# A routing gate moved off TensorE in an attention and two-layer mixture kernel, with a new order for the attention stage

## The chip, the cores and the metric

One core of one Trainium2 chip runs the whole program. The metric is the device time of one execution in microseconds (us). The engines are TensorE (PE, with its weight loads listed as PEld), VectorE (DVE), ScalarE (ACT), GpSimd (POOL) and the DMA queues that SyncE (SP), ScalarE and GpSimd fill.

## What is computed

```python
attn = softmax(rot(q) @ rot(k).T / 8) @ v          # 4 batches, 8 heads, 576 positions, 64 wide
x = attn, as 2304 tokens x 512
logits = x @ w_gate + modality_bias[modality_id]   # 8 experts
x = gate_w * (relu(x @ w1[e]) @ w2[e])             # e = argmax per token, hidden size 1024
do = x @ moe2_w_skip > 0
logits2 = x @ moe2_w_gate                          # 8 columns, with the skip column 9
out = x + do * gate_w2 * (relu(x @ w1b[e2]) @ w2b[e2])
```

Everything is float32. The first mixture (moe1) computes every token, the second (moe2) only those whose skip product is positive. Which tokens go to which expert is known only on the chip.

## The kernel before

**Attention.** Sixteen pairs of heads go through a software pipeline. Every step of it (loads, rotation, transposes, scores, exponentials, products) is a small function, and `attention` gives each a place from the table `POS` (lines 39 to 82): place = 10 x pair + offset. All steps are sorted by place and issued in that order, so the table sets the order in every engine's queue. GpSimd does the rotation (`rope`, L330 to L336), the residues of v (L347) and, every four pairs, the routing of one batch for moe1 (`route1` to `route4p`) and five indirect scatters into the list of moe1 (`scatter1`, L807). Constants are steps too: `constants1` loads the modality bias to one partition (`mbr`, L230) and `constants2` spreads it to 128 partitions with a GpSimd `partition_broadcast` (L240). `moe1_ahead1` to `moe1_ahead3` pick the expert with most tokens, load its first weights into `raw1` and gather the first tokens. Matrix products split each float32 operand into a rounded part and a residue: "hi" on ScalarE, "lo" on VectorE.

**moe1.** Blocks of 256 tokens, two by certain choice, then a list in DRAM order of experts; 9 blocks always run, the rest under nested run-time branches (`nest`, L1288). Here ten run. `body(i)` (L1212) does on TensorE: four groups of the first product (`mm1`, L1094, 24 matmuls each into one of two `psM` banks), the second product of half 0 (`mm2`, L1143, 24 matmuls into `psY`), the transposes of the next block's tokens (`xt`, L1073), the second product of half 1. Each group of `mm1` is followed by relu on ScalarE (L1102) and its residue on VectorE (L1107). Weights of a new expert are split by L982/L986 (first matrix) and L995/L998 (second) when the expert changes.

**The second gate** is `epi(i, t, stage)` for half t of block i. Stage 0 scales `psY` to `x2` on ScalarE (L1160) and takes index, validity and token number on GpSimd (L1161 to L1163). Stage 1 transposes `x2` in four TensorE transposes (L1168), copies them (L1170) and scatters `x2` to `out`. Stage 2 multiplies with the 9 gate columns in four float32 matmuls (L1176, eight PE instructions) and finds the expert on VectorE (L1178 to L1190). Stage 3 counts with two small matmuls (L1193, L1194). Stage 4 computes the slot (L1197 to L1205) and scatters token and weight into the list of moe2. Half 0 runs its stages within its own block, between the pieces of `mm2` of half 1. Half 1 runs them in the next block, one after each group of `mm1`; for the last block they run in the first block of moe2 (`last`).

**moe2** takes blocks of 128 tokens (L1367, L1407), ten here: four of one expert, then one per expert nearly. It has two slots of raw weights, `slots2 = [(raw1, raw2), (raw1b, raw2b)]`. The first expert's weights go to slot 1 on ScalarE's queue during block `sure - 2` of moe1 (`moe2_load`), the second expert's to slot 0 on SP's queue in the last block of moe1 (`moe2_second`, L1334).

Of the kernel before, what the change touches and what calls it, by code (L numbers as in the profile page):

```python
# [39 lines left out]
    load=-36.7017, rope0=-33.9451, rope1=-30.111, v_hi=-21.4821, v_lo=-18.1897,  # L40
    qk_tr0=(-30.6061, -30.6042, -30.5936, -30.1223), qk_tr1=(-28.4904, -28.4904, -28.4848, -28.4848),
    qk_tr2=(-29.2463, -29.2463), qk_hi0=-29.4052, qk_hi1=-27.2491, qk_hi2=-29.202, qk_lo0=-29.1934, qk_lo1=-26.9027,
    qk_lo2=-28.9941, stackq=-25.8754, stackk=-23.011, stack2=-22.5711,
    s_mm0a=(-22.0577, -22.0577, -22.0577, -22.0577), s_max0a=-21.4825, s_exp0a=-20.8972,
    s_mm1a=(-21.3076, -21.3076, -21.3076, -21.3076), s_max1a=-20.1346, s_exp1a=-19.5976,
    s_mm2a=(-22.2316, -22.2316, -22.2316, -22.2316), s_max2a=-21.7162, s_exp2a=-21.4126,
    s_mm3a=(-20.5225, -20.5225, -20.5225, -20.5225), s_max3a=-19.2489, s_exp3a=-17.295,
    s_mm0b=(-14.3536, -14.1043, -14.0042, -13.9921), s_max0b=-12.9587, s_exp0b=-12.9046,
    s_mm1b=(-13.0069, -12.9105, -12.9105, -12.9105), s_max1b=-12.8704, s_exp1b=-12.8563,
    s_mm2b=(-15.4526, -15.4526, -15.4386, -15.4386), s_max2b=-14.6158, s_exp2b=-14.0784,  # L50
    s_mm3b=(-16.5055, -16.5055, -16.5055, -16.5055), s_max3b=-15.336, s_exp3b=-15.2119,
# [12 lines left out]
    t_lo1b=-6.1978, pv1b=(-5.2632, -4.5696, -3.9061, -3.5847), t_mm2b=(-11.6405, -11.6405, -11.6405, -11.6405),
    t_hi2b=-11.3076, t_lo2b=-11.3076, pv2b=(-6.5077, -6.5077, -6.2903, -6.172),
    t_mm3b=(-10.8705, -10.8705, -10.8705, -10.8705), t_hi3b=-9.8594, t_lo3b=-9.5279,
    pv3b=(-5.2659, -5.2659, -5.2659, -5.2659), pv4b=(-3.1789, -3.0274), o_evb=-3.008,
    o_mmb=(-2.908, -2.9041, -2.9041, -2.8421, -2.8421), o_normb=-2.5794,
    t_mm4=(-12.3715, -12.3715, -12.3715, -12.3715), t_hi4=-11.4863, t_lo4=-11.4473, r_inv=-4.0473, x_store=-1.9435,
    route1=-0.138, route2=22.2105, route2a=0.0711, route2b=2.3991, route2c=5.809, route2d=6.9931, route2e=3.0369,  # L70
    route2p=7.9451, route3=10.8285, route4=11.1643, route4p=13.5564, scat0=15.9086, scat1=17.0957, scat2=21.6619,
    scat3=22.8497, scat4=24.3127, ahead1=20.7865, ahead2=24.8061, ahead3=26.173, load2=-9.6073, w_hi0=-4.399,
    w_lo0=-2.8576, w_hi1=-10.8843, w_lo1=-10.3037, w_hi2=-3.048, w_lo2=429.3001, w_hi3=-3.3916, w_lo3=-3.1985,
    x_mm0=-2.5275, x_hi0=-2.4128, x_lo0=-2.2031, x_mm1=-2.35, x_hi1=-2.1246, x_lo1=-2.0387, m_mm0=48.2393,
    m_hi0=181.3328, m_lo0=1552.441, m_mm1=611.0564, m_hi1=1628.6892, m_lo1=1629.4085, m_mm2=1553.3863, m_hi2=1625.391,
# [37 lines left out]
class Kernel:  # L113
# [6 lines left out]
    def run(self):  # L120
# [3 lines left out]
        self.lists = [dp.tile([NLIST, 2], F32, name=f"list{i}") for i in range(2)]  # L124
        self.ident = cp.tile([128, 128], F32, name="ident")
# [97 lines left out]
    def constants1(self):  # L223
# [5 lines left out]
        self.mbr = self.wp.tile([1, 2, E], F32, name="mbr", bufs=1)  # L229
        nc.sync.dma_start(self.mbr, self.mb.unsqueeze(0))  # L230
# [37 lines left out]
    def attention(self):  # L268
# [355 lines left out]
        for p in range(NPAIR):  # L624
# [345 lines left out]
    def moe_tiles(self):  # L970
        wp = self.wp

        self.slots2 = [(self.raw1, self.raw2), (wp.tile([128, 4, F], F32, name="raw1b"), wp.tile([128, 8, DM], F32, name="raw2b"))]
# [4 lines left out]
        self.slots["xT"] = [[self.xT0, wp.tile([128, 2, 4, B1], F32R, name="xT1")], 1]  # L978

# [129 lines left out]
    def moe1(self):  # L1109
# [37 lines left out]
        def epi(i, t, stage):  # L1147
# [5 lines left out]
            if stage == 0:  # L1153

                l = q.ls[i][0]
                x2 = s["x2"] = self.rot(f"x2{t}", [128, DM], bufs=1)
                s["ti"] = self.rot(f"ti{t}", [128, 1], I32, bufs=1)
                s["v"] = self.rot(f"ev{t}", [128, 3], bufs=1)
                s["tg"] = self.rot(f"tg{t}", [128, 2], bufs=1)
                nc.scalar.activation(x2, s["y"], AF.Copy, scale=l[:, t, 1:2])  # L1160
                nc.gpsimd.tensor_copy(s["ti"], l[:, t, 0:1])  # L1161
                nc.gpsimd.tensor_scalar(s["v"][:, 0:1], l[:, t, 0:1], float(N), None, op0=ALU.is_lt)
                nc.gpsimd.tensor_copy(s["tg"][:, 0:1], l[:, t, 0:1])  # L1163
            elif stage == 1:
# [7 lines left out]
            elif stage == 2:  # L1172
                v = s["v"]
# [3 lines left out]
                lg, nm, d = tl_("lg", [128, E + 1]), tl_("nm", [128, 1]), tl_("d", [128, E])  # L1177
                nc.vector.tensor_copy(lg, pg[:, 0 : E + 1])  # L1178
# [7 lines left out]
                nc.vector.tensor_reduce(m8, t8, axis=AX.X, op=ALU.max)  # L1186
                nc.vector.tensor_scalar(v[:, 1:2], lg[:, E : E + 1], 0.0, v[:, 0:1], op0=ALU.is_gt, op1=ALU.mult)
# [3 lines left out]
            elif stage == 3:  # L1191
# [3 lines left out]
            else:  # L1195
                v, oh = s["v"], s["oh"]
                nc.vector.tensor_scalar(s["se"], s["se"], 1e-9, None, op0=ALU.add)  # L1197
                nc.vector.reciprocal(s["tg"][:, 1:2], s["se"])
# [7 lines left out]
                self.scatter(self.lists[1], si, s["tg"], E * CAP)  # L1206
# [5 lines left out]
        def body(i):  # L1212
            def load2(c):
# [4 lines left out]
            if more is not None:  # L1218
# [3 lines left out]
                with cmp.Else():  # L1222
                    self.moe2_second()
# [304 lines left out]
```

## Time and profile before

| | us |
|---|---|
| median of 3 runs | 769.93 (769.36 to 770.71) |
| the profiled execution | 767.88 |
| its span, first to last instruction | 766.2 |
| PE busy | 725.8 (95%) |
| DVE busy | 504.0 (66%) |
| ACT busy | 435.3 (57%) |
| POOL busy | 359.4 (47%) |
| mean granted PE clock | 0.975 of full |

Attention fills the span to about 360 us, moe1 from there to about 622 us, moe2 the rest. Busy times are overlapped: matmuls are pipelined, so that a busy PE is one that has work in flight. A wait is the idle time of an engine just before an instruction, and the profile names what ended it.

### The profile page before, as it was taken

To read this page: it belongs to the slowest core of one execution; us is meant where nothing else is said; L and a number is where in the kernel's file an instruction comes from. 1 tells how busy PE (TensorE), PEld (TensorE's weight loads), DVE (VectorE), ACT (ScalarE), POOL (GpSimd) and SP (SyncE) were. 2 spreads that over 40 slices of the span, in tenths; PEclk is the share of its full clock that TensorE was granted. 3 is DMA by queue.
4 is the path that set the end of the run, shared out by engine and by line. 5 is a ranking of instruction groups with operands and counts; after the bars stand their busy time and mean duration, and the time that the engine had idled before them with its cause. 6 is when DMAs were issued, how large, how long until landed. Compare 5 with 4: busy or idle time off the path is not lost. (4 is left out here: it accounts for less than half of the span.)

```text
span 766.2 us, 15348 instructions
## 1 busy us (share of the span) xinstructions
PE 725.8 (95%) x4948; PEld 654.8 (85%) x4948; DVE 504.0 (66%) x1216; ACT 435.3 (57%) x940; POOL 359.4 (47%) x498
## 2 busy tenths in 40 slices
PE   7898999999999999979899999999999979999994
PEld 6797999999999999968799989988998868877773
DVE  6786899988898899984433333323446753589892
ACT  3785888888888888871222222222235542388781
POOL 7728548767876785253343323231434512133233
PEclk8898999999999999999999999999999989999998
DMA  4654554655465544460011101211693301669910
GB/s 139 137 136 121 136 131 120 148 134 134 119 149 131 137 118 102 118 221 1 15 57 42 42 29 49 51 33 38 178 338 146 124 6 40 242 247 316 325 48 20
DMA packets 75199, 92.29 MB, mean 120 GB/s; under 512 B 29440, under 2 KB 50176, under 8 KB 75090
## 3 DMA queue, kind: packets, MB, share of 16 engines
q1 hardware_dynamic: 65938, 73.74, 34.4%
q0 software_dynamic: 7200, 12.46, 5.2%
q10 hardware_dynamic: 1952, 4.85, 2.1%
q8 instruction: 43, 0.70, 0.4%
q14 instruction: 66, 0.54, 0.3%
HBM read 62.11 MB, written 12.95 MB: 98 GB/s over the span
## 5 line engine op out<-in xcount | busy, mean ns | idle before, releaser
L430 PE MATMUL S<-w1s 128*128 128x288 f32 x640 | 124.8, 321 | 3.0 <-DVE w1s L398 1.2
L1143 PE MATMUL psY<-w2s,hT 128*128 128x512 f32 x480 | 119.3, 397 | 0.0
L1094 PE MATMUL psM<-xT,w1s 128*128 128x256 f32 x864 | 112.6, 287 | 0.0
L1094 PEld LDWEIGHTS psM<-xT,w1s 128*128 128x128 f32 x864 | 106.8, 191 | 0.6 <-issue 0.6
L430 PEld LDWEIGHTS S<-w1s 128*128 128x128 f32 x640 | 95.9, 195 | 6.7 <-ACT PP L447 1.6
L1143 PEld LDWEIGHTS psY<-w2s,hT 128*128 128x128 f32 x480 | 87.2, 188 | 16.7
L447 ACT ACTIVATE PP<-S,nm 128x576 f32<-128x576 f32 x128 | 95.8, 748 | 8.0 <-DVE nm L443 7.5
L443 DVE TENSOR_REDUCE nm<-S 128x1 f32<-128x576 f32 x128 | 94.7, 750 | 3.4 <-PE S L430 3.4
L532 DVE TENSOR_TENSOR tl<-T,th 128x512 fp32r<-128x512 f32 x128 | 88.0, 687 | 11.8 <-ACT th L528 8.7
L525 PE MATMUL T<-ident,PP 128*128 128x128 f32 x512 | 87.4, 275 | 1.1 <-DVE w1s L399 0.4
L528 ACT CAST th<-T 128x512 fp32r<-128x512 f32 x128 | 74.8, 584 | 17.5 <-PE T L525 14.9
L559 PE MATMUL O<-th,vh 128*128 128x288 f32 x256 | 74.0, 329 | 0.6 <-ACT os L568 0.5
L1107 DVE SCALAR_TENSOR_TENSOR hT<-psM,hT 128x512 fp32r<-128x512 f32 x36 | 24.9, 690 | 68.6 <-ACT hT L1102 57.8
L1407 PE MATMUL psY<-w2s,hT 128*128 128x512 f32 x240 | 63.8, 403 | 4.3 <-DVE hT L1386 4.3
L1367 PE MATMUL psM<-w1s,xT 128*128 128x512 f32 x240 | 62.4, 408 | 4.5 <-DVEq L1290 4.5
L525 PEld LDWEIGHTS T<-ident,PP 128*128 128x128 f32 x512 | 63.1, 141 | 3.6 <-DVE tl L532 0.8
L1102 ACT ACTIVATE hT<-psM 128x512 fp32r<-128x512 f32 x36 | 21.5, 598 | 74.1 <-PE psM L1094 73.6
L559 PE MATMUL O<-tl,vh 128*128 128x288 f32 x256 | 61.7, 306 | 0.0
L961 POOL DMA_INDIRECT list<-tg,si x20 | 20.2, 1008 | 85.7 <-issue 56.2
L1367 PEld LDWEIGHTS psM<-w1s,xT 128*128 128x128 f32 x240 | 45.0, 193 | 14.7 <-ACTq L1290 4.6
L1407 PEld LDWEIGHTS psY<-w2s,hT 128*128 128x128 f32 x240 | 43.0, 188 | 15.3 <-DVE hT L1386 6.9
L330 POOL TENSOR_TENSOR mem_w<-qkn,mem_w 128x640 f32<-128x640 f32 x30 | 47.0, 1568 | 19.1 <-PE T L367 11.9
(263 smaller groups left out, 1413.9 us busy)
## 6 DMA issues: line engine op xcount, KB each, us to landing
raw<-in_moe_w_dram SPq DMA_DIRECT2D x20, 512.0 KB
mem_w<-in_moe_w_dram SPq DMA_DIRECT2D x20, 512.0 KB
w1s<-w1s SPq DMA_DIRECT2D x30, 256.0 KB
raw1b<-in_moe_w_dram SPq DMA_DIRECT2D x12, 512.0 KB
raw2b<-in_moe_w_dram SPq DMA_DIRECT2D x12, 512.0 KB
w1s<-w1s SPq DMA_DIRECT2D x16, 288.0 KB
qkn<-in_q_dram SPq DMA_DIRECT2D x16, 256.0 KB
qkn<-in_k_dram SPq DMA_DIRECT2D x16, 256.0 KB
```

Of the source, the lines that this page charges most:

```text
L330: eng.tensor_tensor(r, x, tb[:, i, 0].unsqueeze(1).broadcast_to([128, 2, 5, D]), op=ALU.mult)
L430: yield nc.tensor.matmul(ps[:, hf, 0:288], s["wide"][:, o : o + 128], s["K"][h % 2][:, kk, hf * 288 : hf * 288 + 288], start=first and kk ...
L443: nc.vector.tensor_reduce(st[h // 2]["nm"][:, h % 2, c : c + 1], hs[h]["ps", c][:, :, 0:288], axis=AX.XY, op=ALU.max, negate=True)
L447: nc.scalar.activation(PP[:, c, h % 2 * S : h % 2 * S + S].rearrange("p (a b) -> p a b", a=2), hs[h]["ps", c][:, :, 0:288], AF.Exp, bias=s ...
L525: yield nc.tensor.transpose(ps[:, c * 128 : c * 128 + 128], PP[:, c, o : o + 128], ident)
L528: nc.scalar.copy(hs[h]["th"][:, j, 0:512], hs[h]["tp", j])
L532: nc.vector.tensor_tensor(s["tl"][:, j, 0:512], s["tp", j], s["th"][:, j, 0:512].bitcast(F32), op=ALU.subtract)
L559: yield nc.tensor.matmul(s["ot"][:, hf, 0:288], st[h // 2]["vh"][:, h % 2, j].rearrange("p s d -> p (s d)"), w[:, hf * 288 : hf * 288 + 28 ...
L1094: self.nc.tensor.matmul(ps[:, a], self.w1s[:, wi, dc, fs], x[:, xi, dc], start=(dc == 0 and wi + xi == 0), stop=(dc == 3 and wi == 1))
L1143: nc.tensor.matmul(ps, h[:, hi, f, t * 128 : t * 128 + 128], w2s[:, wi, f], start=(f == 0 and hi + wi == 0), stop=(f == 7 and hi == 1))
L1367: nc.tensor.matmul(ms[hf], x[:, xi, dc], w1s[:, wi, dc, hf * 512 : hf * 512 + 512], start=(dc == 0 and wi + xi == 0), stop=(dc == 3 and xi ...
L1407: nc.tensor.matmul(y, hT[:, hi, f], w2s[:, wi, f], start=(f == 0 and hi + wi == 0), stop=(f == 7 and hi == 1))
```

## The change

1. **Second gate off TensorE.** At the start of moe1 `gate_rows` transposes the 9 gate columns into rows (four TensorE transposes, one ScalarE copy), stores them in DRAM (`wgt`) and loads each row back spread over 128 partitions: 9 DMAs on SP's queue, 256 KB each. Eight of the rows lie in `raw1b`, the ninth in a new tile. For each half of each block the 9 sums over 512 columns are then made by three engines: 3 by a GpSimd product and a ScalarE sum, 6 by a VectorE instruction that multiplies `psY`, the gate weight and a row and gives the sum out. Only half 1 of the last block keeps transposes and matmuls ("turn", "gate"), in moe2.
2. **Later.** Half 0 now makes its last sums, its choice and its list entry in the next block too, half 1 its list entry one step later still.
3. **Copies.** Index, token number and gate weight are copied by ScalarE (two copies, and one more for the list entry); validity moves to VectorE.
4. **Weight slots.** `slots2 = [(raw1b, raw2), (raw1, raw2b)]`. `moe2_load(0, ...)` is gone: the first expert's first matrix goes to `raw1` and the second's second matrix to `raw2` in the last block of moe1 (`moe2_last_loads`), the second's first matrix to `raw1b` in moe2's first block.
5. **Bias by DMA.** The modality bias is loaded straight to 128 partitions; the `partition_broadcast` is gone.
6. **New order.** All of `POS` has new offsets, and the first load of moe1 (`load1`) is a step of its own.

```diff
-    load=-36.7017, rope0=-33.9451, rope1=-30.111, v_hi=-21.4821, v_lo=-18.1897,
+    load=-40.2545, rope0=-39.1031, rope1=-38.1966, v_hi=-28.3147, v_lo=-23.8684,
...
-    scat3=22.8497, scat4=24.3127, ahead1=20.7865, ahead2=24.8061, ahead3=26.173, load2=-9.6073, w_hi0=-4.399,
+    scat3=16.9444, scat4=19.5742, ahead1=14.2223, ahead2=19.7233, ahead3=29.4759, load1=14.5742, load2=-24.2645,
...
-        self.mbr = self.wp.tile([1, 2, E], F32, name="mbr", bufs=1)
-        nc.sync.dma_start(self.mbr, self.mb.unsqueeze(0))
+        self.mbb = self.wp.tile([128, 2, E], F32, name="mbb", bufs=1)
+        nc.sync.dma_start(self.mbb, self.mb.unsqueeze(0).broadcast_to([128, 2, E]))
...
-        nc.gpsimd.partition_broadcast(self.mbb, self.mbr)
...
+        self.slots2 = [(raw1b, self.raw2), (self.raw1, raw2b)]
+        self.gw = [raw1b.rearrange("p c f -> p (c f)")[:, e * DM : e * DM + DM] for e in range(E)]
...
+    def gate_rows(self):
+        nc = self.nc
+        ps = self.bank("G")
+        for c in range(4):
+            nc.tensor.transpose(ps[0 : E + 1, c * 128 : c * 128 + 128], self.wg2s[:, c], self.ident)
+        t = self.rot("x2t", [128, 4, 128])[0 : E + 1].rearrange("p c t -> p (c t)")
+        nc.scalar.copy(t, ps[0 : E + 1])
+        nc.sync.dma_start(self.wgt, t)
+        for e in range(E + 1):
+            nc.sync.dma_start(self.gw[e], self.wgt[e : e + 1].broadcast_to([128, DM]))
...
+            elif stage == "prod":
+                s["prod"] = [self.rot("x2t", [128, 4, 128]).rearrange("p c t -> p (c t)") for _ in range(2)]
+                s["prod"].append(self.rot("prod", [128, DM], bufs=1))
+                for j, w in enumerate(s["prod"]):
+                    nc.gpsimd.tensor_tensor(w, s["x2"], self.gw[j], op=ALU.mult)
+                    if j == 0:
+                        self.scatter(self.out, s["ti"], s["x2"], N)
+            elif stage == "sums":
+                for j, w in enumerate(s["prod"]):
+                    nc.scalar.activation(w, w, AF.Copy, accum_out=s["lg"][:, j : j + 1])
+            elif isinstance(stage, tuple):
+                for e in stage:
+                    nc.vector.scalar_tensor_tensor(
+                        self.junk, s["y"], s["tg"][:, 1:2], self.gw[e], op0=ALU.mult, op1=ALU.mult, accum_out=s["lg"][:, e : e + 1]
+                    )
...
             for g in range(4 if i else 0):
                 mm1(i, g)
-                if i == sure - 2:
-                    self.moe2_load(0, g)
-                epi(i - 1, 1, g + 1)
+                if g == 0:
+                    before(0, "sums", (6, 7, 8))
+                    before(1, "prod")
+                elif g == 1:
+                    before(0, "top")
+                    before(1, (3,))
+                elif g == 2:
+                    before(1, (4, 5))
+                else:
+                    before(0, "count", "list")
+                    before(1, "sums", (6, 7, 8), "top")
...
             mm2(i, 0, range(0, 8))
-            epi(i, 0, 0)
+            epi(i, 0, "meta")
+            epi(i, 0, "out")
             xt(i + 1, 0)
             xt(i + 1, 1)
+            epi(i, 0, "prod")
             mm2(i, 1, range(0, 2))
-            epi(i, 0, 1)
+            before(1, "count", "list")
+            epi(i, 1, "meta")
             load2(0)
             mm2(i, 1, range(2, 4))
-            epi(i, 0, 2)
+            epi(i, 0, (3, 4, 5))
...
+            last(1, "out")
+            last(0, "sums", (6, 7, 8), "top")
             if i == 0:
                 split2(0, range(0, 4))
             mm1(0, range(0, 2))
-            last(1)
+            last(1, "turn")
+            if i == 0:
+                self.moe2_second()
...
-            last(2)
+            last(0, "count", "list")
+            last(1, "gate", "top")
```

`before(t, ...)` runs stages of half t of block i - 1, and `last(t, ...)` those of half t of moe1's last block, in moe2's first one.

## Rows read from the trace of the kernel before

**Rows 1.** Busy time by stretch: a steady part of attention, moe1's blocks, moe2's first, a later one.

```profile
core 0: us, PE busy (x) PEld busy (x) DVE busy (x) ACT busy (x) POOL busy (x), PEclk, DMA share, GB/s
100.00:150.00 50.00, 50.00 (x398) 47.53 (x397) 45.56 (x92) 43.23 (x104) 34.59 (x54) 1.00 0.53 130
...
360.46:376.28 15.82, 13.52 (x71) 11.17 (x71) 3.48 (x13) 3.39 (x8) 6.28 (x11) 1.00 0.01 1
376.28:404.04 27.76, 27.76 (x182) 25.38 (x182) 13.33 (x65) 5.71 (x13) 9.84 (x16) 0.94 0.15 49
404.04:562.67 158.63, 158.10 (x1084) 143.68 (x1083) 55.31 (x252) 38.67 (x85) 52.59 (x89) 1.00 0.24 71
562.67:590.41 27.74, 26.99 (x187) 24.33 (x187) 13.85 (x43) 10.89 (x19) 11.97 (x15) 1.00 0.64 228
590.41:621.80 31.39, 26.65 (x184) 23.96 (x183) 18.75 (x56) 14.91 (x27) 13.66 (x18) 0.96 0.30 98
621.80:637.81 16.01, 16.01 (x75) 13.08 (x75) 9.16 (x27) 7.89 (x16) 3.19 (x4) 0.86 0.03 2
...
680.00:700.00 20.00, 18.34 (x90) 14.43 (x89) 16.78 (x23) 15.26 (x24) 4.78 (x5) 1.00 0.94 339
```

**Rows 2.** Waits of PE: line, what it waited for, us in total, times, longest.

```profile
PE psM L1367 <- DVEq L1290: 4.5, 1, 4.5
...
PE T L367 <- POOL mem_w L336: 3.8, 1, 3.8
PE psG L1193 <- DVE oh L1190: 2.3, 1, 2.3
```

**Rows 3.** Timeline of GpSimd, 44 to 64 us: start, us, instruction, idle before.

```profile
44.56 1.57 POOL L336 TENSOR_TENSOR mem_w<-mem_w 128x640 f32<-128x640 f32 x1
51.94 0.29 POOL L240 PARTITION_BROADCAST mbb<-mbr  x1 [5.81 <-issue]
...
59.23 1.54 POOL L330 TENSOR_TENSOR mem_w<-qkn,mem_w 128x640 f32<-128x640 f32 x1 [6.84 <-PE T L525]
```

**Rows 4.** Busy time by stretch, columns of rows 1: behind PE's wait, and at attention's end.

```profile
64.07:69.40 5.33, 5.33 (x23) 5.20 (x24) 2.19 (x5) 3.19 (x8) 5.25 (x5) 0.50 0.28 76
338.95:346.30 7.35, 4.61 (x23) 3.98 (x24) 5.82 (x11) 5.32 (x10) 3.60 (x7) 0.77 0.48 173
```

**Rows 5.** PE and PEld busy in six steady blocks, of L1168 alone, then of L1176 alone.

```profile
404.04:562.67 158.63, 7.19 (x48) 5.43 (x48) 1.00 0.24 71
...
404.04:562.67 158.63, 11.46 (x96) 12.16 (x96) 1.00 0.24 71
```

**Rows 6.** Timeline of weight loads in block 2: one group of `mm1`, one half of `mm2`.

```profile
411.12 2.94 PEld L1094 LDWEIGHTS psM<-xT,w1s 128*128 128x128 f32 x24
...
417.01 5.34 PEld L1143 LDWEIGHTS psY<-w2s,hT 128*128 128x128 f32 x24
```

**Rows 7.** Groups by line and shape: count, busy us and mean ns, idle before.

```profile
L998 DVE TENSOR_TENSOR w2s<-raw2b,w2s 128x512 fp32r<-128x512 f32 x8 | 5.0, 686 | 6.1 <-ACT w2s L995 6.1
...
L986 DVE TENSOR_TENSOR w1s<-raw1b,w1s 128x1024 fp32r<-128x1024 f32 x4 | 4.7, 1226 | 0.3 <-ACT w1s L982 0.3
...
L1183 ACT ACTIVATION_READ_ACCUMULATOR e_ex<-e_d 128x1 f32 x18 | 3.4, 187 | 0.0
...
L1458 DVE SCALAR_TENSOR_TENSOR x<-psY,list,xh 128x512 f32<-128x512 f32 x2 | 1.5, 750 | 1.5 <-PE psY L1407 1.5
...
L177 POOL TENSOR_TENSOR IIg<-ident 128x512 f32<-128x512 f32 x1 | 1.3, 1260 | 0.0
```

**Rows 8.** Timeline of the last block of moe1 and moe2's first: GpSimd beside VectorE, then PE.

```profile
606.22 4.68 DVE L986 TENSOR_TENSOR w1s<-raw1b,w1s 128x1024 fp32r<-128x1024 f32 x4 [0.26 <-ACT w1s L982]
...
607.63 1.08 POOL L1162 TENSOR_SCALAR ev<-list 128x1 f32<-128x1 f32 x1
...
620.18 0.22 POOL L1162 TENSOR_SCALAR ev<-list 128x1 f32<-128x1 f32 x1
...
631.31 1.63 PE L1407 MATMUL psY<-w2s,hT 128*128 128x512 f32 x6
```

More of the change, by code (lines that the diff above doesn't have):

```diff
@@ L46 @@
[L46 to L51, printed above, removed]
@@ new lines @@
+    qk_tr2=(-35.5703, -35.5703), qk_hi0=-35.957, qk_hi1=-34.3626, qk_hi2=-35.507, qk_lo0=-35.509, qk_lo1=-34.3303,
+    qk_lo2=-35.4693, stackq=-30.1381, stackk=-30.0982, stack2=-25.509,
+    s_mm0a=(-29.1183, -29.1183, -28.9408, -28.9408), s_max0a=-27.5667, s_exp0a=-27.1082,
+    s_mm1a=(-27.658, -27.4021, -27.3816, -27.3816), s_max1a=-26.9413, s_exp1a=-26.9313,
+    s_mm2a=(-29.2907, -29.2907, -29.2907, -29.2907), s_max2a=-28.5991, s_exp2a=-28.0836,
+    s_mm3a=(-27.0942, -27.0942, -27.0896, -26.5376), s_max3a=-25.7889, s_exp3a=-24.5167,
@@ new lines @@
+    s_mm0b=(-21.3933, -21.3218, -21.2364, -21.1351), s_max0b=-20.8898, s_exp0b=-20.1501,
+    s_mm1b=(-20.265, -20.265, -20.265, -20.265), s_max1b=-20.0834, s_exp1b=-20.0491,
+    s_mm2b=(-23.1397, -22.8759, -22.4974, -21.9517), s_max2b=-21.7647, s_exp2b=-21.2057,
+    s_mm3b=(-23.6054, -23.6054, -23.6054, -23.6054), s_max3b=-22.8573, s_exp3b=-21.7306,
+    s_mm4=(-25.509, -25.509, -25.509, -25.509, -25.509, -25.509, -25.509, -25.509), s_max4=-24.5095, s_exp4=-23.3429,
+    l_mma=(-19.9277, -19.8564, -19.8547, -19.8547, -19.8547), l_hia=-19.7903, l_loa=-19.5979,
@@ L83 @@
+    warm3=-41.014, warm4=2082.9893, switch=-10.1407,
 )
@@ L1054, in moe1_ahead2 @@
         self.load(self.raw1, q.w[0], q.e)
+    def moe1_ahead2(self):
+        q = self.q1
         for i in range(NA1):
@@ L1151, in tl_ @@
                 return self.rot("e_" + name, shape, dt)
-            if stage == 0:
+            if stage == "meta":
                 l = q.ls[i][0]
[L1156 to L1164, printed above, removed]
+                for name, w, dt in (("v", 3, F32), ("tg", 2, F32), ("lg", E + 1, F32), ("ti", 1, I32)):
+                    s[name] = self.rot(f"{name}_{t}", [128, w], dt, bufs=1)
+                nc.scalar.copy(s["tg"], l[:, t])
+                nc.scalar.copy(s["ti"], l[:, t, 0:1])
+            elif stage == "out":
+                s["x2"] = self.rot(f"x2{t}", [128, DM], bufs=1)
+                nc.scalar.activation(s["x2"], s["y"], AF.Copy, scale=s["tg"][:, 1:2])
+            elif stage == "prod":
[13 more added lines that the diff above has]
+                    )
+            elif stage == "turn":
                 x2 = s["x2"]
@@ L1171, in epi @@
                 self.scatter(self.out, s["ti"], x2, N)
-            elif stage == 2:
-                v = s["v"]
+            elif stage == "gate":
                 pg = self.bank("G")
@@ L1190, in epi @@
                 nc.vector.tensor_scalar(s["oh"], self.w8, m8, None, op0=ALU.is_equal)
-            elif stage == 3:
+            elif stage == "count":
                 pr = s["pr"] = self.bank("G")
@@ L1212, in body, with before @@
         def body(i):
+            def before(t, *stages):
+                for stage in stages if i else ():
+                    epi(i - 1, t, stage)
             def load2(c):
@@ L1222, in body @@
                 with cmp.Else():
-                    self.moe2_second()
+                    self.moe2_last_loads()
+            before(1, "out")
             if i > 0:
@@ L1292, in nest @@
                     nest(i + 1)
-        self.last = dict(eps[sure - 1, 1])
+        self.last = [dict(eps[sure - 1, t]) for t in range(2)]
         nest(sure)
-        eps[-1, 1] = self.last
+        for t in range(2):
+            eps[-1, t] = self.last[t]
     def moe2_ahead(self):
@@ L1332, in moe2_load, with moe2_last_loads @@
         self.load(q.slots[1][which], q.w[which], e, self.nc.scalar, (c,))
+    def moe2_last_loads(self):
+        q = self.q2
+        self.load(q.slots[1][0], q.w[0], self.reg(q.first["meta"][0:1, 0:1], [ET.SP], E - 1))
+        self.load(q.slots[0][1], q.w[1], self.reg(self.e2, [ET.SP], E - 1))
     def moe2_second(self):
         q = self.q2
-        for i in range(2):
-            self.load(q.slots[0][i], q.w[i], self.reg(self.e2, [ET.SP], E - 1))
+        self.load(q.slots[0][0], q.w[0], self.reg(self.e2, [ET.SP], E - 1))
     def moe2_xt0(self):
@@ L1386, in h_tr, with last @@
                 nc.vector.tensor_tensor(hT[:, 1, fs], p4, hT[:, 0, fs].bitcast(F32), op=ALU.subtract)
-            def last(stage):
-                if i == 0:
-                    self.epi(-1, 1, stage)
+            def last(t, *stages):
+                for stage in stages if i == 0 else ():
+                    self.epi(-1, t, stage)
             def split1(pieces):
@@ L1424, in body @@
             relu(1)
-            last(3)
+            last(1, "count")
             if i > 0:
@@ L1430, in body @@
             mm2(range(0, 2))
-            last(4)
+            last(1, "list")
             if i == 0:
```

89 lines of the change are left out of this document (44 added, 45 removed).

## The prediction

> **What bounds the kernel now.** I read the busy time by stretch first. In attention PE has work in flight for all of 50 us at the full granted clock, 1.00 or 2.4 GHz, while VectorE is busy 45.56 and ScalarE 43.23 [rows 1]. In six steady moe1 blocks PE is busy 158.10 of 158.63 us, 26.44 a block, with VectorE at 55.31 and ScalarE at 38.67 [rows 1]: PE sets the pace, VectorE and ScalarE idle for two thirds. Moe2's later blocks are another case: in 20 us PE is busy 18.34, VectorE 16.78, the DMA engines 0.94 of the time [rows 1], so no engine there has room and the change puts no work there.
>
> Next the waits of PE, which show where it isn't the bound. There are few: 4.5 us at moe2's first product, 3.8 at a transpose of the rotation, 2.3 at the first count [rows 2]. The chain of waits that ended last runs through moe2's scatters and gathers and says little of moe1, which lies before it.
>
> **The change part by part.** The sum is made against the profiled execution, 767.88 us (span 766.2 and 1.7 outside it); the median of the runs is 769.93, 2.05 above.
>
> *Bias by DMA.* GpSimd ends a rotation at 46.13, stands still for 5.81 us before the broadcast, which takes 0.29, and begins the next rotation only at 59.23, after 6.84 us more of idleness [rows 3]. The wait of that second gap is put down to PE, but it follows the only broadcast of the program and the rotation's next steps hang on nothing newer that I can find, so I count both gaps to it: 13.1 us of GpSimd. PE pays for that with 3.8 us of wait [rows 2], and then works 5.33 us at a granted clock of 0.50, the 1.2 GHz level [rows 4]: at 2.4 GHz half of that, 2.7. Attention has no slack behind it, so 3.8 + 2.7 = 6.5 us go. The DMA in its place is one more descriptor set in SP's queue at a point where its data is needed tens of us later: nothing.
>
> *New order.* PE's own order hardly changes and PE is saturated, so the steady part stays. At its end, the weights of moe1 are asked for earlier. The 7.35 us from 338.95 on have PE busy for 4.61 at a mean clock of 0.77 [rows 4]: at most 2.74 of idleness and 0.23 x 7.35 = 1.7 of slow clock, 4.4 us, can go; at least nothing. I take 2.0, under half, since the gathers and the last head stay in the same places of their queues. A new stall in the pipeline is a rival.
>
> *The gate off TensorE.* In six blocks the twelve transposed halves take 5.43 us of weight loads at L1168 and 12.16 at L1176 [rows 5]; the weight loads follow each other without a gap, so they measure what PE gives up: 17.6 us, 2.93 a block, 1.47 a half. Some of it overlaps its neighbours, so I take 2.84 a block. What remains is four groups of 2.94, two halves of 5.34 [rows 6] and about 1.1 of transposes: 23.5.
>
> Can VectorE carry it? The nearest row to the new sum is L1458, the same instruction over 512 columns from PSUM and SBUF, 0.75 us [rows 7]; reading an accumulator is seen on ScalarE alone, 0.19 [rows 7]. I take 0.94, with 0.75 and 1.50 as bounds. Twelve a block are 11.3 us on 9.2 (55.31 / 6): 20.2 of 23.5 after the copies that leave. GpSimd gets six products of 1.26 [rows 7] on 8.8 (52.59 / 6): about 15.5. ScalarE gets six sums and small copies, about 5 on 6.4. All fit. The dates fit too: relu's residue of a group, the three sums behind it and the choice are done before PE wants the `psM` bank back two groups later, and the sums of half 1 are done some 0.9 us before `mm2` of the next half 1 needs their `psY` bank. That is thin: from 1.2 us a sum on, PE would wait.
>
> The Trainium skill, VectorE: DVE Perf Modes, section "Two Vector instructions with no wait between them", says that a Vector instruction that also writes out its accumulator counts as two. No row here shows one. With 0.75 in place of 0.94 the time below would be 2 us less.
>
> So the steady six blocks give 6 x 2.84 = 17.0. The first block (15.82 us, PE busy 13.52 [rows 1]) loses one half's gate, 1.4, and the 2.3 wait for the choice [rows 2], and gains four transposes for the gate rows, 0.4: 3.3. The row DMAs, 2.3 MB, land behind `mm2` of half 0 and are wanted only by VectorE and GpSimd; the block list, 4.1 us of VectorE (13.33 against 9.2 [rows 1]), queues behind their sums, and the second block's first residue behind it. The second block (27.76 [rows 1]) saves 2.84 and the cool clock after the old wait (1.3 above the steady 26.44), and I give 2 back for the list and for a gather not yet landed: 2.1.
>
> *Blocks 8 and 9,* where weights are split, are the dear place. VectorE is busy there 13.85 + 18.75 = 32.6 us of 59.1 [rows 1], and 24 sums of 0.94 make it 55.2, where PE needs 47. So VectorE is the bound, and 55 is the least. I walked its queue: the first matrix's split (4 x 1.23), the transposed tokens' residue, three sums, the second matrix's split (8 x 0.69 [rows 7]) stand in front of block 9's first residue, and PE waits 1.9 and 3.5 us; at the end the split for moe2 stands in front of the sums, and VectorE leaves moe1 some 60 us after block 8 began. At moe1's branch exit all engines meet; today PE starts 1.4 us after GpSimd's last rows, at 621.80 [rows 8]. With that, 61.0 against 59.1: 1.9 lost, between 8 gained (if the split hides) and 7 lost.
>
> *Moe2's first block* now begins with sums and a choice on VectorE (3 x 0.94 + 1.5) ahead of the second matrix's split (8 x 0.69), then a list entry, another choice and a residue: 12.5 us to the first `mm2`, which today starts 9.5 after the exit (631.31 - 621.80 [rows 1, 8]): 3.0 lost.
>
> *Slots, queues.* SP's loads in the last block are as many as before, two in place of two, and ScalarE sheds four issues. The second expert's first matrix comes some 35 us later, into a time with the DMA engines at 0.03 [rows 1], and is wanted in the fourth block: nothing. Scatters of `x2` wait behind one GpSimd product; behind them stand list scatters that only moe2 reads.
>
> Sum: 6.5 + 2.0 + 3.3 + 2.1 + 17.0 - 1.9 - 3.0 = 26.0. 767.88 - 26.0 = 741.9; with 2.05 for the median, **744.0 us**.
>
> **The rivals.**
>
> *PE waits in the gaps.* The gate's transposes and matmuls also covered the residues' latency between groups. If half of the steady gain comes back as waits on `psM` or `psY` banks, 8.5: 752.5 us. For it the margin of 0.9 us; against it two thirds of VectorE idle.
>
> *The splits and GpSimd's products shut each other out.* Beside L986, which reads SBUF twice, a small GpSimd instruction took 1.08 us, without it 0.22 [rows 8]. Six products of 1.26 in blocks 8 and 9 that hold VectorE's splits: 7.5 us, 751.5. The Trainium skill, SBUF - State Buffer, section "SBUF: two separate sides", speaks of an exclusive lock between a GpSimd operation and a VectorE one with two SBUF inputs; the row of 1.08 agrees, and none here shows a split held by a product. For the steady blocks it is nothing, their sums read one operand from PSUM.
>
> *The order moves the stall.* GpSimd's broadcast gap goes but another step of the new order makes PE wait as long: 750.5 us. For it, the gaplessness of today's steady part, which an order can only lose; against, the nearly equal queues.
>
> *Slower: the sums make VectorE the bound everywhere.* Place: `body`, nine blocks of twelve sums. A block then takes 8.9 + 12 s us for a sum of s; nine of them, 20.8 for the splits, 3.0 in moe2, less 8.5 in attention and 3.3 in the first block, against 245.5 today [rows 1], come out even at s = 1.42 us. At twice the row, 1.50, it is 8.6 slower: 778.5 us. For it only that no row shows this instruction with a sum; against it 0.75 for its twin.
>
> **How the numbers follow.** The forecast has 0.60, the bank waits 0.10, the shut-out 0.10, the moved stall 0.07, the slow sums 0.05; 0.08 is for edges that hide more than I think, near 735. The range 734 to 753 takes in both bounds of the splits, the order's 0 to 4.4 and the first three rivals. A measurement of this kernel tells 0.2%, 1.5 us, from no change: faster 0.94, same 0.01, slower 0.05.
>
> **What would show it.** No broadcast and no gap in GpSimd near 46 us, no wait at L367. L1168 and L1176 with 4 and 8 instructions in place of 80 and 160. Steady blocks of 23.5 us with PE still without gaps, sums near 0.94, VectorE 20 a block. Waits of PE for residues behind the splits, and a longer one at moe2's start. It is wrong if the sums take over 1.2 us, if steady blocks stay near 26, or if attention ends later than today less 6.

## The result, and the profile after

After: **775.39 us** median of 8 runs (772.78 to 778.07), the kernel before beside it 770.08 (8 runs). Ratio 1.0071, interval 1.0048 to 1.0093: slower by 0.7%, where 744.0 had been forecast. The profiled execution took 772.98 (span 771.3) against 767.88, 5.1 us more.

| part (profiled executions, us) | before | after | difference | predicted |
|---|---|---|---|---|
| attention, to block 0's first `mm2` | 360.49 | 355.45 | -5.0 | -8.5 |
| block 0 | 15.81 | 11.93 | -3.9 | -3.3 |
| block 1 | 27.76 | 35.01 | +7.3 | -2.1 |
| blocks 2 to 6 | 132.36 | 118.88 | -13.5 | -14.2 |
| block 7 | 26.66 | 29.40 | +2.7 | -2.8 |
| blocks 8 and 9, with the exit | 58.72 | 71.30 | +12.6 | +1.9 |
| moe2 | 144.4 | 149.3 | +4.9 | +3.0 |

A block is counted from its first `mm1` to that of the next; the rows of before are [rows 1] with slightly other borders. The busy time by stretch of after, blocks 1, 3, 7, 8 and 9 (columns as in [rows 1]):

```profile
367.38:402.39 35.01, 26.68 (x157) 24.11 (x156) 28.77 (x84) 10.13 (x30) 20.34 (x21) 0.85 0.20 72
...
426.10:449.69 23.59, 23.59 (x158) 21.30 (x156) 21.61 (x68) 9.70 (x30) 15.88 (x15) 1.00 0.15 46
...
521.27:550.67 29.40, 25.93 (x162) 22.91 (x162) 23.78 (x88) 9.97 (x31) 18.43 (x20) 0.94 0.29 68
550.67:577.73 27.06, 24.05 (x160) 21.56 (x158) 19.89 (x58) 13.64 (x35) 11.33 (x11) 1.00 0.62 230
577.73:621.97 44.24, 25.63 (x158) 22.83 (x157) 39.31 (x91) 17.41 (x42) 22.08 (x19) 0.86 0.35 113
```

The steady block is the one that was forecast: 23.59 us, PE without a gap. In the others PE's own work takes 24 to 27 us, longer where the granted clock (PEclk) is lower: 26.68 us at 0.85 in block 1, 25.93 at 0.94 in block 7, 25.63 at 0.86 in block 9. The rest is waiting. PE's waits in after, against [rows 2]:

```profile
PE psM L1115 <- DVE hT L1128: 20.9, 4, 8.3
PE psM L1429 <- DVEq L1346: 9.8, 1, 9.8
PE psY L1469 <- DVE hT L1448: 4.5, 5, 0.9
PE T L364 <- DVE w1s L399: 2.3, 1, 2.3
PE psG L1233 <- DVE oh L1230: 2.2, 2, 2.0
```

The broadcast's wait is gone. New are 20.9 us for relu's residue (L1128): 8.3 in block 1, 1.5 in block 7, 3.0 in block 8, 8.1 in block 9; and 9.8 at moe1's exit. So the question is what VectorE did before those residues. In block 1:

```profile
368.22 0.75 DVE L1198 SCALAR_TENSOR_TENSOR junk<-psY,tg,raw1b 128x512 f32<-128x512 f32 x1 [4.47 <-DMA raw1b<-wgt]
...
372.04 1.76 DVE L878 TENSOR_TENSOR b_t<-o_after,b_nb 128x64 f32<-128x64 f32 x1
...
374.25 3.21 DVE L907 SCALAR_TENSOR_TENSOR b_off<-b_beg,f_done 128x8 f32<-128x8 f32 x1
...
380.84 0.67 DVE L1128 SCALAR_TENSOR_TENSOR hT<-psM,hT 128x512 fp32r<-128x512 f32 x1
```

GpSimd in that time:

```profile
370.08 0.93 POOL L808 DMA_INDIRECT list<-g_tg,g_si  x1 [6.91 <-DMA raw1b<-wgt]
...
372.41 1.31 POOL L1189 TENSOR_TENSOR x2t<-x,raw1b 128x512 f32<-128x512 f32 x1
373.89 1.02 POOL L962 DMA_INDIRECT out_dram<-x,ti  x1 [0.17 <-issue]
374.94 1.27 POOL L1189 TENSOR_TENSOR x2t<-x,raw1b 128x512 f32<-128x512 f32 x1
376.16 1.27 POOL L1189 TENSOR_TENSOR prod<-x,raw1b 128x512 f32<-128x512 f32 x1
```

A step on 8 columns (L907; 0.15 us in before) takes 3.21 us and ends as the products end. A second thing is in the first rows of both: the sums and a list scatter wait for the gate rows' DMAs. In block 9 a step of the list entry and the split of the second matrix (a like one takes 5.0 us for eight in [rows 7]) lie in front of the residue:

```profile
579.11 3.29 DVE L1244 TENSOR_TENSOR acc<-acc,oh 128x8 bf16<-128x8 bf16 x1
...
584.90 7.03 DVE L1016 TENSOR_TENSOR w2s<-mem_w,w2s 128x512 fp32r<-128x512 f32 x8
591.85 0.68 DVE L1128 SCALAR_TENSOR_TENSOR hT<-psM,hT 128x512 fp32r<-128x512 f32 x1
```

In block 7, which begins at 521.27, GpSimd makes the first product 13.7 us after the block's start (6.9 in block 3). The choice on VectorE then waits for ScalarE's sum of the last product, and PE for the choice:

```profile
534.94 1.32 POOL L1189 TENSOR_TENSOR x2t<-x,raw1b 128x512 f32<-128x512 f32 x1
...
540.74 1.27 POOL L1189 TENSOR_TENSOR prod<-x,raw1b 128x512 f32<-128x512 f32 x1
```

```profile
542.80 0.16 DVE L1218 TENSOR_REDUCE e_nm<-lg 128x1 f32<-128x8 f32 x1 [3.20 <-ACT prod L1194]
```

```profile
544.45 0.17 PE L1233 MATMUL psG<-oh,U 128*128 128x8 bf16 x1 [1.99 <-DVE oh L1230]
```

### The profile page after: what moved, and what is told of

The parts are those of the page before. It is cut to its first block, busy times and chain, and to the rows that moved or that the text cites. A ratio compares the mean times of both kernels' runs of the same rounds, so it can differ in the third digit from the quotient of the medians.

```text
span 771.3 us, 15293 instructions
## 1 busy us (share of the span) xinstructions
PE 705.4 (91%) x4724; PEld 637.7 (83%) x4724; DVE 623.5 (81%) x1445; ACT 473.3 (61%) x1096; POOL 414.2 (54%) x494
## 5 line engine op out<-in xcount | busy, mean ns | idle before, releaser
L430 PE MATMUL S<-w1s 128*128 128x288 f32 x640 | 134.1, 323 | 4.0 <-ACT w1s L386 1.3
L1115 PE MATMUL psM<-xT,w1s 128*128 128x256 f32 x864 | 109.9, 289 | 21.6 <-DVE hT L1128 20.9
L430 PEld LDWEIGHTS S<-w1s 128*128 128x128 f32 x640 | 98.7, 192 | 8.7 <-ACT PP L447 1.7
L532 DVE TENSOR_TENSOR tl<-T,th 128x512 fp32r<-128x512 f32 x128 | 88.0, 688 | 12.6 <-ACT th L528 8.0
L525 PE MATMUL T<-ident,PP 128*128 128x128 f32 x512 | 94.3, 274 | 0.8 <-DVE w1s L399 0.4
L528 ACT CAST th<-T 128x512 fp32r<-128x512 f32 x128 | 75.1, 587 | 17.8 <-PE T L525 14.9
L1198 DVE SCALAR_TENSOR_TENSOR junk<-psY,tg,raw1b 128x512 f32<-128x512 f32 x95 | 71.0, 747 | 10.2 <-DMA raw1b<-wgt 5.1
L559 PE MATMUL O<-th,vh 128*128 128x288 f32 x256 | 76.4, 332 | 0.9 <-ACT os L568 0.9
L1429 PE MATMUL psM<-w1s,xT 128*128 128x512 f32 x240 | 64.6, 417 | 10.0 <-DVEq L1346 9.8
L1189 POOL TENSOR_TENSOR x2t<-x,raw1b 128x512 f32<-128x512 f32 x38 | 51.8, 1363 | 31.3 <-ACT x L1183 28.6
L559 PE MATMUL O<-tl,vh 128*128 128x288 f32 x256 | 64.5, 305 | 0.0
L334 POOL TENSOR_TENSOR mem_w<-qkn,mem_w 128x320 f32<-128x320 f32 x60 | 51.0, 874 | 0.0
```

The source lines that it names most:

```text
L430: yield nc.tensor.matmul(ps[:, hf, 0:288], s["wide"][:, o : o + 128], s["K"][h % 2][:, kk, hf * 288 : hf * 288 + 288], start=first and kk ...
L525: yield nc.tensor.transpose(ps[:, c * 128 : c * 128 + 128], PP[:, c, o : o + 128], ident)
L528: nc.scalar.copy(hs[h]["th"][:, j, 0:512], hs[h]["tp", j])
L532: nc.vector.tensor_tensor(s["tl"][:, j, 0:512], s["tp", j], s["th"][:, j, 0:512].bitcast(F32), op=ALU.subtract)
L559: yield nc.tensor.matmul(s["ot"][:, hf, 0:288], st[h // 2]["vh"][:, h % 2, j].rearrange("p s d -> p (s d)"), w[:, hf * 288 : hf * 288 + 28 ...
L1115: self.nc.tensor.matmul(ps[:, a], self.w1s[:, wi, dc, fs], x[:, xi, dc], start=(dc == 0 and wi + xi == 0), stop=(dc == 3 and wi == 1))
```

## The experiments

Theory 1: GpSimd's products hold VectorE's instructions that read SBUF twice, and ScalarE's sums wait for products. Theory 2: VectorE's load and the order of its queue. Theory 3: the attention order. Block times of all kernels, as above (blocks 2 to 6 as a mean). A row comes from the one profiled execution, which can lie off the median: 759.19 us for 754.11 with "blocks 0 to 5", 765.35 for 770.63 with "list first".

| | first `mm2` | 0 | 1 | 2 to 6 | 7 | 8 | 9 |
|---|---|---|---|---|---|---|---|
| before | 360.5 | 15.8 | 27.8 | 26.5 | 26.7 | 27.3 | 31.4 |
| after | 355.5 | 11.9 | 35.0 | 23.8 | 29.4 | 27.1 | 44.2 |
| bias alone | 357.7 | 15.6 | 26.2 | 26.5 | 26.7 | 27.4 | 31.4 |
| bias, order | 352.8 | 16.6 | 27.8 | 26.5 | 26.7 | 27.3 | 33.0 |
| all sums on VectorE | 351.2 | 11.9 | 33.6 | 25.9 | 27.7 | 31.3 | 40.4 |
| list first | 351.0 | 11.9 | 32.5 | 23.7 | 29.2 | 27.0 | 44.6 |
| loads on SP | 353.3 | 11.9 | 36.3 | 23.7 | 27.8 | 26.9 | 45.2 |
| no products | 352.1 | 11.9 | 31.5 | 23.7 | 23.9 | 27.5 | 35.8 |
| 2 of 12 VectorE sums | 353.6 | 11.9 | 29.5 | 23.7 | 29.9 | 25.7 | 35.4 |
| blocks 1 to 5, old order | 353.6 | 13.8 | 24.8 | 23.8, block 6 25.8 | 26.6 | 27.6 | 31.4 |
| blocks 1 to 5, new order | 353.2 | 13.8 | 24.8 | 23.8, block 6 25.8 | 26.6 | 27.6 | 32.1 |
| blocks 0 to 5 | 357.7 | 11.9 | 37.1 | 23.7, block 6 25.8 | 26.6 | 27.3 | 31.3 |
| the same, 0 on VectorE | 356.5 | 11.9 | 31.3 | 23.7, block 6 25.8 | 26.6 | 27.4 | 31.7 |
| blocks 1 to 6, later loads | 355.1 | 14.9 | 24.7 | 23.8 | 31.6 | 34.4 | 32.4 |

**Bias alone**, in the kernel before:

```diff
-        nc.sync.dma_start(self.mbr, self.mb.unsqueeze(0))
+        nc.sync.dma_start(self.mbb, self.mb.unsqueeze(0).broadcast_to([128, 2, E]))
...
-        nc.gpsimd.partition_broadcast(self.mbb, self.mbr)
```

> The kernel before with the bias DMA alone (part 5 of the change). By the prediction: the wait of 3.8 us at the rotation's transpose and the slow clock behind it (2.7) go, 6.5 us less, about 763.5 us, and attention reaches the first mm2 near 354.0 instead of 360.46. Rival: GpSimd's gap of 13 us is not the broadcast's but a queue that would have waited anyway; then the stall stays or moves a few us on and the time is within 1.5 us of before.

760.32 us (4 runs) against 768.32 of before (13 runs): ratio 0.9891 (0.9865 to 0.9917), 8.0 us less. The first rival is out.

**Bias and order**: the same with the new `POS` and `load1`.

> The kernel before with the bias DMA, the new order and the first load as a step of its own (parts 5 and 6), the gate still on TensorE. By the prediction the order is worth 2.0 more than the bias alone: 8.5 us less than before, 761.4. By the trace of after, attention as a whole gained only 5.0 (first mm2 at 355.45 against 360.46); if that holds here, 765. If it is slower than the bias alone, the order is a loss in itself. If moe1 from its first mm2 to moe2 takes the 261 us of before, attention's order has nothing to do with moe1's loss.

761.65, ratio 0.9908 (0.9874 to 0.9943): not to be told from the bias alone. Blocks 2 to 8 are the same to a tenth; blocks 0, 1 and 9 are 1.0, 1.5 and 1.7 us longer in its profiled execution. Theory 3 is out as the cause of the loss, and the order's 2.0 did not show. After stood 5.3 us above before, this stands 6.7 below: parts 1 to 4, the gate's move with its later stages, copies and slots, cost 12.0. No run takes these four apart.

**All sums on VectorE**, in after:

```diff
-                    nc.gpsimd.tensor_tensor(w, s["x2"], self.gw[j], op=ALU.mult)
...
             elif stage == "sums":
-                for j, w in enumerate(s["prod"]):
-                    nc.scalar.activation(w, w, AF.Copy, accum_out=s["lg"][:, j : j + 1])
+                epi(i, t, (0, 1, 2))
```

> After with all nine sums on VectorE, no GpSimd products and no ScalarE sums. Theory 1 (GpSimd's products hold VectorE's instructions with two SBUF operands): the list entries of 1.9 to 3.3 us, the held step of the block list (3.2) and the held split (7.0 for eight) fall to their lengths in before (0.17, 0.15, 4.9), the waits for the products go, and blocks 1, 7 and 9 together lose 8 us or more of their excess; steady blocks rise from 23.6 to about 25, as VectorE goes from 21.6 to that: near 775 in all. Theory 2 (it is VectorE's load and the order of its queue alone): the long ones stay long, and every block grows, 1.5 in the steady ones and 5 in each of 1, 7, 8 and 9: near 800.

782.94, ratio 1.0199 (1.0160 to 1.0238), between the two. Each theory was half right: the held steps fell to their old length, by line and shape in before, in after, then here:

```profile
L1201 DVE TENSOR_TENSOR e_sl<-e_sl,oh 128x8 f32<-128x8 f32 x19 | 3.2, 167 | 0.6
```

```profile
L1243 DVE TENSOR_TENSOR e_sl<-e_sl,oh 128x8 f32<-128x8 f32 x18 | 25.9, 1441 | 0.6
...
L1244 DVE TENSOR_TENSOR acc<-acc,oh 128x8 bf16<-128x8 bf16 x18 | 8.9, 497 | 0.0
L1016 DVE TENSOR_TENSOR w2s<-mem_w,w2s 128x512 fp32r<-128x512 f32 x8 | 7.0, 952 | 0.0
```

```profile
L1016 DVE TENSOR_TENSOR w2s<-mem_w,w2s 128x512 fp32r<-128x512 f32 x8 | 4.9, 684 | 0.0
...
L1237 DVE TENSOR_TENSOR e_sl<-e_sl,oh 128x8 f32<-128x8 f32 x18 | 3.0, 167 | 0.6
...
L1238 DVE TENSOR_TENSOR acc<-acc,oh 128x8 bf16<-128x8 bf16 x18 | 2.8, 155 | 0.0
```

But the steady block grew to 25.9. VectorE is busy for 21.4 of that, so it isn't the bound all through; PE waits for it at two places, 0.96 us for a residue that stands behind six sums and 0.84 us for a `psY` bank.

**Block list first**, in after:

```diff
-            epi(i, 0, (3, 4, 5))
             if i == 0:
...
                 self.seq_load(q, NA1, 0)
+            epi(i, 0, (3, 4, 5))
             load2(1)
```

> After with the block list of block 0 ahead of half 0's sums of columns 3 to 5. Theory 2 (order of VectorE's queue): the list no longer waits for the row DMAs (sums waited 4.5 + 0.7 us for them), the second block's first residue comes 4 to 5 us earlier, PE's wait of 8.3 us there falls to about 3, and with the clock that stays high 5 to 7 us go: 769. Theory 1 alone: the list is held by the products wherever it stands, 2 us or less.

770.63 (10 runs), ratio 1.0027 (1.0000 to 1.0054): of after's 5.3 us above before some 3 went (the intervals overlap), block 1 lost 2.5. Half the size expected: with the list out of the way the residue waits 5.02 us for ScalarE's relu, which stands behind a sum that waits for a late product. ScalarE and VectorE in this kernel:

```profile
372.02 0.63 ACT L1194 ACTIVATE x2t<-x2t 128x512 f32<-128x512 f32 x1 [5.47 <-POOL x2t L1189]
...
376.36 0.58 ACT L1123 ACTIVATE hT<-psM 128x512 fp32r<-128x512 f32 x1
```

```profile
376.98 0.69 DVE L1128 SCALAR_TENSOR_TENSOR hT<-psM,hT 128x512 fp32r<-128x512 f32 x1 [5.02 <-ACT hT L1123]
```

**Steady blocks only**, in after, with the old order, slots and loads. `here` runs a stage for blocks in `ENG`, `alone` the stages of before, at their old places, for the others:

```diff
+        ENG = (1, 2, 3, 4, 5)
...
-                for stage in stages if i else ():
+                for stage in stages if i - 1 in ENG else ():
...
-            epi(i, 0, "prod")
+            here(0, "prod")
             mm2(i, 1, range(0, 2))
...
+            alone(i, 0, "turn")
```

> The kernel before with the bias DMA and the old order; the gate leaves TensorE in blocks 1 to 5 alone, and blocks 0, 6 to 9 and moe2 keep transposes and matmuls, old slots and old loads; the gate rows are loaded at the end of block 0. Theory (the gate's move is worth 2.7 us in a steady block and all of its loss is made by the blocks around): the bias alone gave 760.3; five blocks by 2.7 less, 746.8, with blocks 7, 8 and 9 at 26.7, 27.4 and 31.4 as before. Rival (moving it costs in every block, through held instructions): steady blocks above 24.5, 752 or more.

**745.45**, ratio 0.9716 (0.9660 to 0.9771): faster than both kernels, and near the 746.8 that was expected. PE's waits in moe1 of this kernel are these alone, the exit's 4.6 among them:

```profile
PE psM L1442 <- DVEq L1365: 4.6, 1, 4.6
PE psT L1205 <- DVE xT L1100: 1.0, 1, 1.0
PE psG L820 <- DVE acc L1243: 0.5, 1, 0.5
PE psG L1232 <- DVE oh L1229: 0.3, 1, 0.3
```

**The same in the new order**:

> The same with the new order. With the bias alone the new order made 761.65 of 760.3, no difference that the runs could tell: 747 to 748. If the order of the attention stage were worth the 2.0 of the prediction: 745.

746.19, ratio 0.9729 (0.9674 to 0.9784): again no difference.

**Block 0 too**: `ENG` with 0, `gate_rows` at the start of moe1.

> The same with the new order, and block 0 too has its gate on the engines, with the rows loaded at the start of moe1 as in the change. It prices the first block alone. Theory (rows landing among the list scatters make GpSimd's products late, the sums stand in front of the block list, the products hold the list): block 0 is 4 us shorter, as in after (11.9 for 15.8 to 16.6), and block 1 grows from about 24 to 33 to 35, so 5 to 7 us slower than the run without: 753. Rival (block 0 pays as the prediction had it, 3.3 less): 744.

754.11, ratio 0.9806 (0.9763 to 0.9849), 7.9 us slower: blocks 0 and 1 together take 49.1 for 38.6 (in an execution of 759.19 us, so that the blocks differ by more than the medians).

**Block 0's sums on VectorE** in that kernel:

```diff
+                    if i > 0:
                         nc.gpsimd.tensor_tensor(w, s["x2"], self.gw[j], op=ALU.mult)
...
+                if i == 0:
+                    epi(i, t, (0, 1, 2))
```

> The run with the new order and the gate of blocks 0 to 5 off TensorE (754.1), but block 0's nine sums a half all on VectorE, no GpSimd product there. Block 1 takes 37.1 us in that run. Theory (GpSimd's late products, behind list scatters that share the DMA engines with the gate rows, keep ScalarE's sums and with them the second group's relu waiting, and hold the block list): block 1 falls to about 31, the whole to 748. Rival (the wait is VectorE's: rows arriving late, sums ahead of the list): block 1 grows by the six extra sums, 3 to 5 us, 758.

Block 1 took 31.3, as theory 1 said, with six more sums on VectorE. The whole, 751.51 (ratio 0.9772, 0.9739 to 0.9806), won 2.6, less than the block and less than the 6 expected; the intervals overlap, and the 37.1 is from the execution of 759.19 us. Without a product 31.3 is still 6.6 more than the 24.7 of the kernel that leaves block 0 as it was.

**Loads on SP**, in after: `moe2_load` issues on SP's queue.

> After with the four loads of moe2's second matrix issued by SP in place of ScalarE. ScalarE stood still for 11.1 us at these loads in block 7, and block 8's second residue came 3.0 us late for PE. If that standing still is what delays block 8: block 8 goes from 27.06 to about 24, and the whole by 3: 772.4. If the standing still is hidden (PE waited for something else): 775, within 1.5 us.

772.13 (10 runs), ratio 1.0042 (1.0010 to 1.0074), not to be told from after. ScalarE's standing still went (first after, then this kernel), and `mm1` of block 8 ran without a gap. Blocks 7 to 9 kept their time within 0.9 us (99.9 for 100.7): block 8 now waits 1.5 us for a `psY` bank, the exit takes 11.1 for 9.8, and block 9's residue, late by 5.4 us in place of 8.1, finds PE at a mean clock of 0.82 in place of 0.86.

```profile
557.24 0.58 ACT L1097 CAST xT<-psT 128x512 fp32r<-128x512 f32 x1 [11.10 <-DMA raw2b<-in_moe_w_dram]
```

```profile
547.99 0.59 ACT L1097 CAST xT<-psT 128x512 fp32r<-128x512 f32 x1 [3.19 <-PE psT L1094]
```

**No products**: after without products and ScalarE's sums. This run and the next are one execution each, and both leave out columns of the second gate.

```diff
-                    nc.gpsimd.tensor_tensor(w, s["x2"], self.gw[j], op=ALU.mult)
...
-                    nc.scalar.activation(w, w, AF.Copy, accum_out=s["lg"][:, j : j + 1])
...
+            nc.vector.memset(self.rot(f"lg_{t}", [128, E + 1], bufs=1)[:, 0:3], -1e30)
```

> After without GpSimd's products and without ScalarE's three sums; columns 0 to 2 of the second gate are not computed (a constant stands there, so moe2's choice is among five experts, and times behind moe1 are not comparable). VectorE's queue is that of after. Blocks 1, 7, 8 and 9 of after take 35.0, 29.4, 27.1 and 44.2 us. Theory 1 (products hold VectorE and ScalarE): the held list entries fall to 0.17 us and these four blocks to about 28, 26, 25.5 and 36. Theory 2 (VectorE's sums and their place in its queue): each within 2 us of after.

Blocks 1, 7 and 9 lost 3.5, 5.5 and 8.4, block 8 grew by 0.5, against theory 1: 16.9 us less. Blocks 8 and 9 together take 63.4 us here, near the 61.0 forecast, where after takes 71.3. The steady blocks, where PE sets 23.6 either way, show what the products did to VectorE: over blocks 2 to 6 it is busy 17.0 us a block here and 21.2 in after, 4.3 us that slack hides, nearly all of it in small steps that take longer. One such block (the like one of after, above, holds five more instructions of VectorE):

```profile
426.10:449.70 23.60, 23.60 (x157) 21.32 (x157) 16.91 (x63) 6.02 (x18) 7.01 (x8) 1.00 0.15 46
```

**2 of 12 VectorE sums**: after with the sum of column 8 alone on VectorE.

```diff
-                for e in stage:
+                for e in stage[2:] if stage[-1] == E else ():
```

> After with the products and ScalarE's sums, but without VectorE's sums of columns 3 to 7; these columns are not computed (a constant stands there; times behind moe1 are not comparable). One sum a half stays. VectorE loses 10 of 12 sums a block, 8 us. Theory 2: blocks 1, 7, 8 and 9 fall from 35.0, 29.4, 27.1 and 44.2 to about 30, 27, 24.5 and 34. Theory 1: list entries stay held at up to 3 us and the four blocks lose less than 3 us each. If both looks win about half of block 9, the two add up there.

Blocks 1, 8 and 9 lost 5.5, 1.3 and 8.9, block 7 grew by 0.5: 15.2 us less, with the list entries held as in after (26.1 us for 20). In block 9 the two would make 17.2 of the 20.6 that it has above a steady block, if they add up; no run leaves out both.

**Block 6 too, loads later**: `ENG` to 6, first matrix loaded in block 7's second product, second in block 8.

> The run with the old order and the gate of blocks 1 to 5 off TensorE (745.45), with block 6 added and moe2's first weights loaded one step later on ScalarE's queue (first matrix between the pieces of block 7's second product, second matrix in block 8). Block 6 should fall from 25.77 to 23.7; block 7, where moe2's first choice stands in VectorE's queue among block 6's sums, may take 1 to 2 back (29.4 in after, 26.6 here): 743 to 746. It would be a loss, over 748, if ScalarE's loads hold block 8 as in after.

753.94 (6 runs), ratio 0.9800 (0.9769 to 0.9832): 8.5 slower than the 745.45, where 743 to 746 was expected. Block 6 won its 2.0, blocks 7 and 8 grew by 11.9, and PE waits 4.7 us for a copy that stands behind a load on ScalarE. The run changes two things, so it does not say what block 6 alone would do:

```profile
PE psG L1212 <- ACT x2t L1207: 4.7, 1, 4.7
```

## Why the prediction was wrong

The step that failed is the price of the blocks at the edges. For blocks 1, 7, 8 and 9 the sum has 2.1 + 2.8 won and 1.9 lost, 3.0 us won in all; measured were 22.6 lost. These 25.6 us are most of the 31.4 between forecast and result (775.39 - 744.0).

- **Bias by DMA, 6.5**: right, 8.0 in the runs. **New order, 2.0**: did not show. Where attention ends varied from 351.0 to 357.7 us between the profiled executions that share the bias DMA; 5.0 in place of 8.5 lies within that, though "later than today less 6" was one of the prediction's own signs of being wrong.
- **The gate off TensorE, steady**: right. 2.70 us a block for 2.84, 23.6 for 23.5. The sum takes 0.748 + 0.083 = 0.83 us where 0.94 was taken, and it is two instructions, as the Trainium skill says (VectorE: DVE Perf Modes, section "Two Vector instructions with no wait between them"); the trace agrees with the accumulator read as a row of its own, 0.083. The rival that PE waits in the gaps is out for after (with all nine sums on VectorE PE did wait, 1.8 us a block), and so is the one of slow sums.
- **First block**: right, 3.9 for 3.3.
- **Second block, 2.1 won**: failed, 7.3 lost. The 2 us given back for the list should have been 11: sums waiting for gate rows (5.1), the list held (4.6 of its 9.7), GpSimd's products behind a list scatter that waited 6.91 for a row's DMA. The path was in the prediction (the list queues behind the sums, "and the second block's first residue behind it"); its size was wrong: the wait for the rows and the hold stood at nothing. PE's wait of 8.3 us also cost clock: its own work took 26.68 us at a mean clock of 0.85. Without products the block still took 31.5, so they are 3.5 of the miss; what the row DMAs alone cost no run shows.
- **Block 7**, counted as steady: failed, 5.6 off, and nearly all of it the products and their sums (without both 23.9). "All fit" compared busy times and did not walk GpSimd's queue, where two lists and two gathers for moe2 stand in front of the products beside the block's own; VectorE then waits 3.20 us for ScalarE's last sum and PE 2.0 for the choice.
- **Blocks 8 and 9, 1.9 lost**: failed, 12.6. The bound was right in block 9, VectorE (39.31 of 44.24 us), and so was the queue that was walked; its steps were taken at the lengths of a kernel without products. Without them VectorE is busy 9.4 us less in block 9, and both blocks take 63.4 us where 61.0 was forecast.
- **The shut-out** was in the list of rivals with 0.10 and 7.5 us, in blocks 8 and 9 only. Together with ScalarE's sums and their waits for products, which no run takes apart from it, it is worth about half of the miss: 16.9 us in one execution, over blocks 1, 7, 8 and 9. "For the steady blocks it is nothing" is right for the time and wrong for the reason: the sums read one operand from PSUM and none is held (all 114 between 0.729 and 0.753 us), but the small steps around them read SBUF alone, and one such step of the list entry (L1243) took 25.9 us for 18 in place of 3.0.
- **moe2, 3.0 lost**: its first `mm2` comes 13.0 us after the exit, 12.5 were forecast; 4.9 in all. **Slots, queues, nothing**: no run has the new slots alone. The loads left on ScalarE cost nothing that the runs could tell.

What stays open: why ScalarE stands so long at a load (11.1 us at block 7's end, once; the four issues span 5.06 of them), and how much of moe2's 4.9 is the granted clock, 0.75 over the 16 us behind the exit in place of 0.86 [rows 1].

## What to carry to other kernels

Work moved to engines with busy time to spare pays where the bound engine has no gap and the queues repeat; in blocks at the edges, with lists, splits and loads, the same work stands in front of what the bound engine needs, and there the old way can stay: five blocks of ten gave 14.9 us beyond the bias (745.45 against 760.32), all ten, with the slots and copies that came along, cost 12.0. Walk every queue in order, and take a step's length from a trace in which the same engines are at work beside it.

## What the hardware showed that was not expected

- One VectorE step on 128x8, 0.17 us without products, ends only as GpSimd's whole row of instructions ends: 2.97 us in block 7 of after, through a scatter and two products.

```profile
546.92 2.97 DVE L1243 TENSOR_TENSOR e_sl<-e_sl,oh 128x8 f32<-128x8 f32 x1
```

```profile
546.29 1.01 POOL L962 DMA_INDIRECT out_dram<-x,ti  x1 [0.16 <-issue]
547.34 1.28 POOL L1189 TENSOR_TENSOR x2t<-x,raw1b 128x512 f32<-128x512 f32 x1
548.57 1.28 POOL L1189 TENSOR_TENSOR prod<-x,raw1b 128x512 f32<-128x512 f32 x1
```

- It goes both ways: a product that overlaps a split of VectorE took 2.25 us for 1.3.

```profile
576.25 1.22 DVE L1004 TENSOR_TENSOR w1s<-raw,w1s 128x1024 fp32r<-128x1024 f32 x1
```

```profile
576.37 2.25 POOL L1189 TENSOR_TENSOR x2t<-x,raw1b 128x512 f32<-128x512 f32 x1 [6.25 <-ACT x L1183]
```

- The Trainium skill, SBUF — State Buffer, section "SBUF: two separate sides", has the lock for the length of one instruction. The trace agrees with a lock, and shows a step of VectorE that stays out over two products in a row.
- At attention's end (330 to 340 us), where both run the same code, after was granted a mean clock of 0.66, a mix of the levels of 1.2 and 2.4 GHz, and the kernel with the list first 1.00. PE had been busy for 8.9 of the 10 us before in both; no run says why they differ.
